# Weight conversion in 32-bit words, a planner that holds the buffers of accumulating DMAs, and 14 weight blocks converted early and kept in DRAM

## The chip, the cores and the metric

One Trainium2 chip, one core of it. The metric is the device time of one execution in microseconds, the median of several runs. Three runs of the kernel before took 594.22, 595.67 and 596.27 us.

## What is computed

Three blocks follow each other on 1536 rows (2 batches of 768) of 512 values. Everything is float32; the weights arrive as float64 numbers, since the host hands their 64 bits over as int64.

```python
# attention: local window of 16, plus 24 block summaries (max of k, mean of v over 32 rows)
scores_all = concat([where(|i-j|<16, q@k.T/8, -1e9), q@k_sum.T/8 + log(32)])
x = softmax(scores_all) @ concat([v, v_sum])        # 8 heads of 64
# first block
h = x @ w_in                                        # 512 -> 2048
x = (maximum(h, 0) + log1p(exp(-abs(h)))) @ w_out   # 2048 -> 512
# second block
out = ((x @ w1) * (x @ w2)) @ w3 @ w_out2           # 512 -> 1024 -> 1024 -> 512
```

## The kernel before

**Numbers and products.** A float32 operand is kept as two fp32r halves, high and low, and each product is three matmuls (`PASSES`, L18; `mm3`, L221). A matmul here is 128x128 by 128x512. The second and third rows chunk of the H and AB products go through a seven-product scheme (`prod`, L666; `keep`, `plus`). `w3 @ w_out2` is multiplied out on the chip first (`w34_mm`, tile `wps`), written to DRAM (`w_d`) and read back.

**Stages.** Attention runs to about 68 us. Then the H and X products (tiles `hps`, `abps`, `xps`, 68 to 354 us in the trace), with softplus between them on DVE and ACT (`S_a` to `S_lo`, L465 to L480), then `w3 @ w_out2` (333 to 396 us, interleaved with the last X products), then the second block (AB, `ops`).

**Weight conversion, one block of 128x512 float64 at a time.** There are 72 blocks (`jobs`): 16 of `w_in`, 16 of `w_out`, 8 of `wo2`, 16 of `w3`, 16 of `w1` and `w2`. SP loads 512 KB into a tile `raw` of 128 x 512 x 2 int32 (`load`, L229): pool `st` with three buffers, or pool `g` for every other block of wo2 and w3. Then:

- `conv_a` (L235): the top three mantissa bits of the low word are moved to the bottom of it. It reads every fourth uint16 and writes every fourth uint16; on ACT (L240, 69 blocks) or DVE (L238, the first 3).
- `conv_b` (L242, DVE L244): the sign bit is put into the neighbouring uint16.
- `conv_c` (L246): high word times a power of two into a tile `cv` (pool of five); ACT (L250) or DVE (L252).
- `conv_d` (L254, DVE L256): shift and bitwise or of `cv` and `raw`; here the `raw` buffer becomes free.
- `conv_e` (L258, ACT L260) and `conv_f` (L262, POOL or DVE L264): high and low half.

**X sums.** Sixteen steps of w_out do not fit one accumulation in PSUM, so four groups of four are copied out to a tile `xo` (`X_copy`, L491: odd ones on ACT, even ones on DVE), and stored to DRAM tile `x_d`: the first group by a plain DMA on SP, the three others by an accumulating DMA issued from POOL (`X_sum`, L498; 36 of them). `X_load` (L506, SP L509) reads the sum back as `x2f`. `xo`, the softplus `tm` and others share a pool `tmp` of four buffers.

**Order.** Nothing is scheduled by hand. Each step is given to a planner, class `Order`, with engine, cost, place, needs and the buffers that it takes and gives back. `order()` lists the steps engine by engine with its own clock and writes each engine's instruction order, which the chip then keeps to. SP issues its DMAs in that order: a DMA that has to wait holds up those behind it. In the planner a buffer that `X_sum` reads is free 0.3 us after the POOL instruction (`LAT`, L22), and `X_load` is ready then. Step names: `l` load, `ca` to `ce` and `c` the conversion, `Xo` copy, `Xs` sum, `Xl` load of the sum, `wm` the w3 product.

The jobs of wo2 and w3 have their conversion placed from `Ph5_7`, late in the H and X stage, on (L891). `X1_6_0` and `X2_15_0` are names of X steps: second rows chunk with block 6, and the last X step of the third chunk.

Of the kernel before, what the change touches and what calls it, by code (L numbers as in the profile page):

```python
# [19 lines left out]
class Order:  # L20
# [9 lines left out]
        self.owner = {}  # L30
        self.extra = {}

    def add(self, name, eng, cost, place, fn, needs=(), take=(), give=(), port=None, table=None, lead=0.0):
        assert name not in self.steps, name
        self.steps[name] = (eng, cost, place, fn, list(dict.fromkeys(d for d in needs if d)), list(take))
        self.extra[name] = (eng == "POOL" if port is None else port, table, lead)
# [62 lines left out]
    def order(self):  # L99
# [25 lines left out]
        while len(out) < len(st):  # L125
            best = None
            for eng, ns in wait.items():
                free = busy_to.get(eng, 0.0)
                cand = []
                for n in ns:  # L130
                    t = max(free, ready[n])
                    port, tab, _ = self.extra[n]
# [30 lines left out]
            port, tab, _ = self.extra[n]  # L163
            if tab:
                table = tab
            for tag, b in take:
                slots[tag].remove(min(slots[tag]))
                head[tag] += 1
            end[n] = t + cost
            busy_to[eng] = end[n]  # L170
            if port:
                port_to = end[n]
            out.append((t, len(out), n))
            for b in gives.get(n, ()):
                slot_end[b] = max(slot_end.get(b, 0.0), end[n] + self.LAT[eng])
                open_users[b] -= 1
                if not open_users[b]:
                    slots[self.owner[b]].append(slot_end[b])
            for m in after[n]:
                lat = self.LAT[eng] if st[m][0] != eng else 0.0 if eng == "PE" else self.SAME  # L180
                ready[m] = max(ready.get(m, 0.0), end[n] + lat)
                left[m] -= 1
                if not left[m]:
                    wait.setdefault(st[m][0], {})[m] = 1
# [6 lines left out]
def fused_kernel(ctx, tc, q, k, kwin, v, vb, w_in, w_out, w1, w2, w3, wo2, mask, sel, ident, out):  # L191
# [43 lines left out]
    def conv_a(kind, i, eng):  # L235
        r = raws[kind, i]
        if eng == "DVE":
            nc.vector.tensor_scalar(r.bitcast(U16)[:, :, 0], r.bitcast(U16)[:, :, 1], 13, None, ALU.logical_shift_right)  # L238
        else:
            nc.scalar.activation(r.bitcast(U16)[:, :, 0], r.bitcast(U16)[:, :, 1], AF.Copy, bias=-(0.5 - 2.0 ** -14), scale=2.0 ** -13)  # L240

    def conv_b(kind, i):  # L242
        r = raws[kind, i]
        nc.vector.tensor_scalar(r.bitcast(U16)[:, :, 1], r.bitcast(U16)[:, :, 3], 0x8000, None, ALU.bitwise_and)  # L244

    def conv_c(kind, i, eng):  # L246
        c = cvs[kind, i] = cv_p.tile([P, D], I32, tag="cv", name="cv")
# [242 lines left out]

    def X_copy(c, g, o):  # L491
        xo[c, g, o] = tmp_p.tile([P, CH], F32, tag="tmp", name="xo")
        if o % 2:
# [258 lines left out]
    for u in range(T):  # L752
# [131 lines left out]
    early = set(jobs[:EARLY])  # L884
    first2 = set(jobs[:3])
    conv_on = lambda j: "DVE" if j in early or j[0] in ("wo2", "w3") and j[1] % 2 else "ACT"
    for j in jobs:
        kind, i, p = j
        n, pl = f"{kind}{i}", at_job[j]
        if kind in ("wo2", "w3"):  # L890
            pl = max(pl, at_["Ph5_7"] + 1.2 * (jobs.index(j) - 32))  # L891
        rt = "g" if kind in ("wo2", "w3") and jobs.index(j) % 2 else "st"
        add("l" + n, "SP", 2.0, pl - 6, lambda kind=kind, i=i, rt=rt: load(kind, i, rt), ("swap" if rt == "g" else None,), [(rt, "r" + n)])
        eng = conv_on(j) if j in first2 else "ACT"
        add("ca" + n, eng, .43 if eng == "DVE" else .66, pl, lambda kind=kind, i=i, eng=eng: conv_a(kind, i, eng), ("l" + n,), port=eng == "DVE")
# [295 lines left out]
```

## Time and profile before

| | us |
|---|---|
| median of three runs | 595.67 |
| the three runs | 594.22 to 596.27 |
| the profiled execution | 592.06 |
| its span, first to last instruction | 590.2 |

Engines' busy share of the span: PE 93%, DVE 73%, ACT 61%, POOL 30%. The mean granted TensorE clock is 0.976 of full speed. The profiled execution is 3.6 us shorter than the median; differences are read from its trace. In the trace a PE row with a bracket shows how long PE sat idle before that row and which engine's instruction ended the wait. A PE that is busy is not always at pace: matmuls that run at the lower clock take twice as long, so a stretch is best read by how many matmuls it holds.

### The profile page before, as it was taken

The numbers are of one execution on the slowest core, as the hardware profiler recorded it, in microseconds if no ns is written. First come the engines' busy times: TensorE is split into PE (matmuls) and PEld (weight loads), VectorE is DVE, ScalarE is ACT, GpSimd is POOL, SyncE is SP. The second block draws the span as 40 slices with busy tenths as digits, with TensorE's granted clock in tenths as the row PEclk, the third lists the DMA queues.
The fourth block names the chain that finished last, engine by engine and source line by source line (L and its number), as shares of the span: only waits on it lengthen the run. The fifth ranks groups of instructions, "written<-read, shape, count | busy, mean of one in ns | idle before, by whom it ended". The sixth has DMA issues, their size and how long they took to land.

```text
span 590.2 us, 8684 instructions
## 1 busy us (share of the span) xinstructions
PE 548.8 (93%) x3118; PEld 442.3 (75%) x3118; DVE 429.4 (73%) x824; ACT 358.3 (61%) x677; POOL 176.9 (30%) x162
## 2 busy tenths in 40 slices
PE   7778899999999999799999788998999999999997
PEld 4566677888887888578877666786887888888885
DVE  4778998886978879667653856799686998753430
ACT  4789878788466886455642958967876433333220
POOL 2465633127132254302312614225645100000000
PEclk9889999999999999879999789999999999999999
DMA  9998744453126457814557589835534010000021
GB/s 311 274 256 211 190 140 137 150 183 108 72 74 141 106 144 142 197 19 58 165 99 159 128 267 272 265 140 191 154 122 123 1 72 0 1 0 1 2 89 53
DMA packets 31442, 76.93 MB, mean 130 GB/s; under 512 B 4104, under 2 KB 4552, under 8 KB 31400
## 3 DMA queue, kind: packets, MB, share of 16 engines
q1 hardware_dynamic: 26216, 66.95, 36.0%
q0 software_dynamic: 5184, 9.44, 11.1%
q8 instruction: 24, 0.39, 0.3%
q14 instruction: 18, 0.15, 0.1%
HBM read 58.45 MB, written 17.92 MB: 129 GB/s over the span
## 4 chain that ended last, share of the span: by engine, by line
PE 56%; DMA 14%; ACT 9%; issue 8%; DVE 8%; POOL 3%; SPq 0%; POOLq 0%; DVEq 0%; ACTq 0%
PE abps L681 19%; PE xps L223 14%; PE ops L223 9%; PE hps L223 8%; DMA raw<-in_w_dram 6%; DMA x_d<-xo 5%; ACT raw L240 3%; ACT s L394 3%; PE abps L223 2%; POOL w L264 2%; DVE cv L256 2%; DMA raw<-in_w_in_dram 2%; DVE raw L244 2%; ACT w L260 1%; PE z_p L838 1%
## 5 line engine op out<-in xcount | busy, mean ns | idle before, releaser
L223 PE MATMUL xps<-gt,w 128*128 128x512 f32 x576 | 146.9, 404 | 12.9 <-ACT gt L477 6.8
L223 PEld LDWEIGHTS xps<-gt,w 128*128 128x128 f32 x576 | 112.0, 196 | 40.1 <-ACT gt L477 8.3
L264 POOL TENSOR_TENSOR w<-cv,w 128x512 fp32r<-128x512 f32 x60 | 88.0, 1473 | 172.9 <-ACT w L260 159.3
L240 ACT ACTIVATE raw<-raw 128x512 uint16<-128x512 uint16 x69 | 94.3, 1385 | 29.0 <-DMA raw<-in_w_dram 17.7
L223 PE MATMUL hps<-xt,w 128*128 128x512 f32 x288 | 70.1, 394 | 1.3 <-DVE gt L480 1.3
L223 PE MATMUL ops<-w,pt 128*128 128x512 f32 x288 | 69.5, 389 | 1.2 <-DVE pt L579 1.2
L244 DVE TENSOR_SCALAR raw<-raw 128x512 uint16<-128x512 uint16 x72 | 60.5, 840 | 12.5 <-ACT raw L240 12.4
L223 PEld LDWEIGHTS hps<-xt,w 128*128 128x128 f32 x288 | 54.2, 190 | 13.8 <-DVE gt L480 2.1
L223 PEld LDWEIGHTS ops<-w,pt 128*128 128x128 f32 x288 | 54.0, 188 | 12.8 <-DVE pt L579 1.6
L256 DVE SCALAR_TENSOR_TENSOR cv<-cv,raw 128x512 int32<-128x512 int32 x72 | 56.8, 788 | 2.8 <-ACT cv L250 0.2
L260 ACT CAST w<-cv 128x512 fp32r<-128x512 f32 x72 | 44.7, 635 | 18.0 <-DVE cv L256 17.5
L687 ACT COPY u<-abps 128x512 f32<-128x512 f32 x42 | 24.7, 591 | 49.4 <-PE abps L681 46.3
L502 POOL DMA_DIRECT2D x_d<-xo x36 | 32.9, 1028 | 72.7 <-DVE xo L496 56.0
L693 DVE TENSOR_TENSOR u<-u,abps 128x512 f32<-128x512 f32 x42 | 28.9, 687 | 29.1 <-ACT u L687 18.3
L223 PE MATMUL wps<-w 128*128 128x512 f32 x192 | 45.0, 392 | 2.9 <-ACT w L260 2.1
L223 PE MATMUL abps<-x2t,w 128*128 128x512 f32 x192 | 46.1, 393 | 1.7 <-POOL w L264 0.9
L223 PEld LDWEIGHTS wps<-w 128*128 128x128 f32 x192 | 35.7, 188 | 11.9 <-ACT w L260 2.6
L223 PEld LDWEIGHTS abps<-x2t,w 128*128 128x128 f32 x192 | 35.5, 188 | 11.2 <-POOL w L264 2.6
L470 ACT ACTIVATE tm<-tm 128x512 f32<-128x512 f32 x48 | 30.0, 636 | 21.0 <-DVE tm L467 20.7
L681 PE MATMUL abps<-t,s 128*128 128x512 f32 x168 | 42.3, 389 | 0.0
L394 ACT ACTIVATE s<-s,sm 128x120 f32<-128x120 f32 x96 | 36.6, 385 | 7.2 <-DVE sm L388 7.1
L681 PEld LDWEIGHTS abps<-t,s 128*128 128x128 f32 x168 | 31.5, 188 | 6.5
(101 smaller groups left out, 846.7 us busy)
## 6 DMA issues: line engine op xcount, KB each, us to landing
raw<-in_w_dram SPq DMA_DIRECT2D x32, 512.0 KB, 4.0
x_d<-xo POOLq DMA_DIRECT2D x36, 256.0 KB, 5.4
raw<-in_w_in_dram SPq DMA_DIRECT2D x16, 512.0 KB, 3.5
raw<-in_w_out_dram SPq DMA_DIRECT2D x16, 512.0 KB, 4.1
vw<-in_v_dram SPq DMA_DIRECT2D x12, 384.0 KB, 9.8
raw<-in_wo_dram SPq DMA_DIRECT2D x8, 512.0 KB, 5.7
kt<-in_k_dram SPq DMA_DIRECT2D x4, 768.0 KB
qt<-in_q_dram SPq DMA_DIRECT2D x12, 256.0 KB, 5.6
```

The lines of the kernel that those rows point to most:

```text
L223: nc.tensor.matmul(ps, lhs(a), rhs(b), start=first and i == 0, stop=last and i == 2)
L240: nc.scalar.activation(r.bitcast(U16)[:, :, 0], r.bitcast(U16)[:, :, 1], AF.Copy, bias=-(0.5 - 2.0 ** -14), scale=2.0 ** -13)
L244: nc.vector.tensor_scalar(r.bitcast(U16)[:, :, 1], r.bitcast(U16)[:, :, 3], 0x8000, None, ALU.bitwise_and)
L256: nc.vector.scalar_tensor_tensor(c, c, 3, r[:, :, 0], ALU.logical_shift_left, ALU.bitwise_or)
L260: nc.scalar.copy(w[:, 0], f(cvs[kind, i]))
L264: eng.tensor_tensor(w[:, 1], f(cvs[kind, i]), f(w[:, 0]), ALU.subtract)
L394: nc.scalar.activation(s[:, e], s[:, e], AF.Exp, bias=sm[:, 0, e:e + 1], scale=-1.0, accum_out=sm[:, 1, e:e + 1])
L470: nc.scalar.activation(tm[c, i], tm[c, i], AF.Softplus)
L502: nc.gpsimd.dma_start(x2_d[4 * c + o], xo[c, g, o], accum_op=ALU.add)
L681: nc.tensor.matmul(ps, w[:, a, (o + kk) * P:(o + kk + 1) * P], rhs(b), start=k in (1, 5, 2) and kk == 0 and n == 0, stop=kk == 1 and n == ...
L687: nc.scalar.copy(tu[z, j, name], bank[z, j, k])
L693: nc.vector.tensor_tensor(tu[z, j, d], tu[z, j, d], bank[z, j, k], ALU.add)
```

## The change

Three things.

1. `conv_a` and `conv_b` write the whole low 32-bit word instead of single uint16. `conv_a` on ACT still reads the uint16 and writes an int32; on DVE it is a 32-bit shift by 29. `conv_b` takes the sign from the high word and combines it with the low word in one two-input instruction.
2. The planner's `add` takes a `tail`. A step's buffers and followers wait for it in the planner's clock: 4.4 us for the accumulating DMAs, 1.0 us for the plain ones of `X_sum`. The copy's engine is taken from a list `XE`, with the same assignment as before.
3. The first 14 jobs of wo2 and w3 are loaded and taken through `conv_a` to `conv_d` between the planned times of `X1_6_0` and `X2_15_0`, evenly spread. The resulting `cv` tile is stored to DRAM (`park`) and read back into another `cv` tile (`unpark`) 4 us ahead of the old place of the conversion; `conv_e` and `conv_f` stay there. Their `raw` tiles are all in pool `st`.

```diff
     def conv_a(kind, i, eng):
         r = raws[kind, i]
         if eng == "DVE":
-            nc.vector.tensor_scalar(r.bitcast(U16)[:, :, 0], r.bitcast(U16)[:, :, 1], 13, None, ALU.logical_shift_right)
+            nc.vector.tensor_scalar(r[:, :, 0], r[:, :, 0], 29, None, ALU.logical_shift_right)
         else:
-            nc.scalar.activation(r.bitcast(U16)[:, :, 0], r.bitcast(U16)[:, :, 1], AF.Copy, bias=-(0.5 - 2.0 ** -14), scale=2.0 ** -13)
+            nc.scalar.activation(r[:, :, 0], r.bitcast(U16)[:, :, 1], AF.Copy, bias=-(0.5 - 2.0 ** -14), scale=2.0 ** -13)
     def conv_b(kind, i):
         r = raws[kind, i]
-        nc.vector.tensor_scalar(r.bitcast(U16)[:, :, 1], r.bitcast(U16)[:, :, 3], 0x8000, None, ALU.bitwise_and)
+        nc.vector.scalar_tensor_tensor(r[:, :, 0], r[:, :, 1], -0x80000000, r[:, :, 0], ALU.bitwise_and, ALU.bitwise_or)
...
+    def park(kind, i):
+        nc.sync.dma_start(pk_d[kind, i], f(cvs[kind, i]))
+    def unpark(kind, i):
+        cvs[kind, i] = cv_p.tile([P, D], I32, tag="cv", name="cv")
+        nc.sync.dma_start(f(cvs[kind, i]), pk_d[kind, i])
...
-                slot_end[b] = max(slot_end.get(b, 0.0), end[n] + self.LAT[eng])
+                slot_end[b] = max(slot_end.get(b, 0.0), end[n] + self.LAT[eng] + tail)
...
-                lat = self.LAT[eng] if st[m][0] != eng else 0.0 if eng == "PE" else self.SAME
+                lat = self.LAT[eng] + tail if st[m][0] != eng else 0.0 if eng == "PE" else self.SAME + tail
...
+    PACE, AHEAD, EARLY, PARK, PA, PB = 3.2, 6.0, 8, 14, "X1_6_0", "X2_15_0"
+    parked = [j for j in jobs if j[0] in ("wo2", "w3")][:PARK]
+    lo, hi = at_[PA], at_[PB]
...
+        pk = j in parked
+        pl2 = lo + (hi - lo) * parked.index(j) / len(parked) if pk else pl
+        rt = "g" if kind in ("wo2", "w3") and jobs.index(j) % 2 and not pk else "st"
...
-        add("cb" + n, "DVE", .43, pl + .1, lambda kind=kind, i=i: conv_b(kind, i), ("ca" + n,), port=True)
+        add("cb" + n, "DVE", .68, pl2 + .1, lambda kind=kind, i=i: conv_b(kind, i), ("ca" + n,), port=True)
...
+        if pk:
+            add("pk" + n, "SP", .7, pl2 + 3, lambda kind=kind, i=i: park(kind, i), ("cd" + n,), (), ("p" + n,))
+            add("up" + n, "SP", .7, pl - 4, lambda kind=kind, i=i: unpark(kind, i), ("pk" + n,), [("cv", "c" + n)])
...
                 add(f"Xs{n}", "POOL" if g else "SP", 1.1 if g else .7, None, lambda c=c, g=g, o_=o_: X_sum(c, g, o_),
-                    (f"Xo{n}", g and f"Xs{c}{g-1}_{o_}"), (), (f"xo{n}",), lead=4 if g == 3 else 0, port=False)
+                    (f"Xo{n}", g and f"Xs{c}{g-1}_{o_}"), (), (f"xo{n}",), lead=4 if g == 3 else 0, port=False, tail=4.4 if g else 1.0)
```

## Rows read from the trace of the kernel before

**Rows 1.** PE in order of time: start us, length us, instruction, count, idle before.
```profile
304.52 12.40 PE L223 MATMUL xps<-gt,w 128*128 128x512 f32 x54
316.76 1.52 PE L681 MATMUL abps<-t,w 128*128 128x512 f32 x6
...
319.48 4.24 PE L223 MATMUL xps<-gt,w 128*128 128x512 f32 x18
328.02 5.36 PE L223 MATMUL xps<-gt,w 128*128 128x512 f32 x12 [4.30 <-ACT gt L477]
...
349.55 4.87 PE L223 MATMUL xps<-gt,w 128*128 128x512 f32 x12 [2.54 <-ACT gt L477]
354.25 11.04 PE L223 MATMUL wps<-w 128*128 128x512 f32 x48
```

**Rows 2.** Windows: length, busy us (instructions) of PE PEld DVE ACT POOL, PEclk, DMA share, GB/s.
```profile
68.00:91.00 23.00, 21.60 (x122) 16.93 (x121) 22.66 (x36) 16.81 (x24) 9.01 (x8) 1.00 0.38 121
91.00:174.00 83.00, 83.00 (x366) 68.74 (x367) 70.60 (x106) 61.16 (x89) 27.86 (x18) 1.00 0.38 127
174.00:196.00 22.00, 20.67 (x90) 16.38 (x89) 17.89 (x32) 14.85 (x23) 6.76 (x6) 1.00 0.51 98
196.00:226.00 30.00, 30.00 (x134) 24.81 (x133) 23.90 (x40) 23.47 (x37) 14.51 (x13) 1.00 0.64 140
226.00:256.00 30.00, 25.40 (x98) 19.90 (x97) 23.29 (x35) 18.08 (x26) 8.91 (x7) 0.86 0.69 158
256.00:291.00 35.00, 35.00 (x152) 28.90 (x151) 22.68 (x37) 17.33 (x28) 6.14 (x6) 0.98 0.38 84
291.00:323.00 32.00, 31.06 (x137) 25.38 (x137) 17.34 (x29) 12.78 (x19) 7.23 (x8) 1.00 0.61 118
323.00:354.00 31.00, 24.05 (x87) 18.34 (x86) 21.86 (x31) 22.56 (x34) 12.05 (x10) 0.83 0.74 199
354.00:396.00 42.00, 39.12 (x169) 31.12 (x168) 32.87 (x46) 34.19 (x45) 14.00 (x13) 1.00 0.73 222
396.00:453.00 57.00, 54.18 (x233) 42.79 (x232) 44.83 (x51) 42.89 (x63) 29.53 (x19) 1.00 0.50 160
453.00:587.00 134.00, 133.06 (x588) 109.83 (x586) 81.23 (x134) 41.26 (x72) 6.78 (x4) 1.00 0.07 24
```

**Rows 3.** DVE in order of time, around 248 us.
```profile
248.20 0.69 DVE L496 COPY xo<-xps 128x512 f32<-128x512 f32 x1 [5.36 <-DMA x_d<-xo]
```

**Rows 4.** DMAs that touch x_d, from issue to landing.
```profile
DMA to landing us min/median/max: 3.7/5.4/8.7
```

**Rows 5.** ACT in order of time, around 323 us.
```profile
323.67 1.33 ACT L240 ACTIVATE raw<-raw 128x512 uint16<-128x512 uint16 x1 [8.29 <-DMA raw<-in_w_dram]
```

**Rows 6.** Waits of SP's own queue: us in total, times, longest us.
```profile
SPq L509 <- DMA x_d<-xo: 38.8, 7, 14.1
SPq L231 <- PE xps L223: 37.5, 2, 37.1
```

**Rows 7.** SP's queue in order of time, around 316 us.
```profile
316.16 0.47 SPq L231 DMA_DIRECT2D raw<-in_w_dram  x1
```

**Rows 8.** Groups of instructions: count, busy us, mean ns of one, idle before.
```profile
L240 ACT ACTIVATE raw<-raw 128x512 uint16<-128x512 uint16 x69 | 94.3, 1385 | 29.0 <-DMA raw<-in_w_dram 17.7 <-DMA raw<-in_w_out_dram 5.2 <-DMA raw<-in_wo_dram 3.2
L244 DVE TENSOR_SCALAR raw<-raw 128x512 uint16<-128x512 uint16 x72 | 60.5, 840 | 12.5 <-ACT raw L240 12.4
L256 DVE SCALAR_TENSOR_TENSOR cv<-cv,raw 128x512 int32<-128x512 int32 x72 | 56.8, 788 | 2.8 <-ACT cv L250 0.2
L250 ACT ACTIVATE cv<-raw 128x512 f32<-128x512 f32 x52 | 35.7, 692 | 0.0
```

**Rows 9.** DMA issues: count, KB each, median us to landing.
```profile
w_d<-w34o SPq DMA_DIRECT2D x8, 256.0 KB, 4.5
w34r<-w_d SPq DMA_DIRECT2D x8, 256.0 KB, 2.7
```

More of the change, by code (lines that the diff above doesn't have):

```diff
@@ L31, in __init__, with add @@
         self.extra = {}
-    def add(self, name, eng, cost, place, fn, needs=(), take=(), give=(), port=None, table=None, lead=0.0):
+    def add(self, name, eng, cost, place, fn, needs=(), take=(), give=(), port=None, table=None, lead=0.0, tail=0.0):
         assert name not in self.steps, name
         self.steps[name] = (eng, cost, place, fn, list(dict.fromkeys(d for d in needs if d)), list(take))
-        self.extra[name] = (eng == "POOL" if port is None else port, table, lead)
+        self.extra[name] = (eng == "POOL" if port is None else port, table, lead, tail)
         for t, b in take:
@@ L131, in order @@
                     t = max(free, ready[n])
-                    port, tab, _ = self.extra[n]
+                    port, tab, _, tail = self.extra[n]
                     if port:
@@ L162, in order @@
             del wait[eng][n]
-            port, tab, _ = self.extra[n]
+            port, tab, _, tail = self.extra[n]
             if tab:
@@ L214, in fused_kernel @@
     w34_d = dr.tile([8, P, D], F32, name="w34_d")
+    pk_d = {("wo2", i): dr.tile([P, D], F32, name=f"pk_wo2{i}") for i in range(8)}
+    pk_d.update({("w3", i): dr.tile([P, D], F32, name=f"pk_w3{i}") for i in range(16)})
     x2_d = [dr.tile([P, CH], F32, name=f"x2_d{r}") for r in range(12)]
@@ L492, in X_copy @@
         xo[c, g, o] = tmp_p.tile([P, CH], F32, tag="tmp", name="xo")
-        if o % 2:
+        if XE[o] == "ACT":
             nc.scalar.copy(xo[c, g, o], xps[c, g, o])
@@ L762, in fused_kernel @@
     WO = (0, 4, 1, 5, 2, 6, 3, 7, 8, 12, 9, 13, 10, 14, 11, 15)
+    XE = ("DVE", "ACT", "DVE", "ACT")
     SEQ = (1, 5, 6, 2, 7, 4, 3)
@@ L865, in fused_kernel @@
     jobs += [(f"w{m+1}", i, "wo" if i < 3 else ("wi", "g")[m] if i == 3 else "b") for i in range(8) for m in range(2)]
-    PACE, AHEAD, EARLY = 3.2, 6.0, 8
+    PACE, AHEAD, EARLY, PARK, PA, PB = 3.2, 6.0, 8, 14, "X1_6_0", "X2_15_0"
     first = {}
@@ L889, in fused_kernel @@
         n, pl = f"{kind}{i}", at_job[j]
+        pk = j in parked
         if kind in ("wo2", "w3"):
             pl = max(pl, at_["Ph5_7"] + 1.2 * (jobs.index(j) - 32))
-        rt = "g" if kind in ("wo2", "w3") and jobs.index(j) % 2 else "st"
-        add("l" + n, "SP", 2.0, pl - 6, lambda kind=kind, i=i, rt=rt: load(kind, i, rt), ("swap" if rt == "g" else None,), [(rt, "r" + n)])
+        pl2 = lo + (hi - lo) * parked.index(j) / len(parked) if pk else pl
+        rt = "g" if kind in ("wo2", "w3") and jobs.index(j) % 2 and not pk else "st"
@@ L894, in fused_kernel @@
+        add("l" + n, "SP", 2.0, pl2 - 6, lambda kind=kind, i=i, rt=rt: load(kind, i, rt), ("swap" if rt == "g" else None,), [(rt, "r" + n)])
         eng = conv_on(j) if j in first2 else "ACT"
-        add("ca" + n, eng, .43 if eng == "DVE" else .66, pl, lambda kind=kind, i=i, eng=eng: conv_a(kind, i, eng), ("l" + n,), port=eng == "DVE")
-        add("cb" + n, "DVE", .43, pl + .1, lambda kind=kind, i=i: conv_b(kind, i), ("ca" + n,), port=True)
+        add("ca" + n, eng, .43 if eng == "DVE" else .66, pl2, lambda kind=kind, i=i, eng=eng: conv_a(kind, i, eng), ("l" + n,), port=eng == "DVE")
@@ L897, in fused_kernel @@
+        add("cb" + n, "DVE", .68, pl2 + .1, lambda kind=kind, i=i: conv_b(kind, i), ("ca" + n,), port=True)
         eng = conv_on(j)
-        add("cc" + n, eng, .43 if eng == "DVE" else .66, pl + .3, lambda kind=kind, i=i, eng=eng: conv_c(kind, i, eng),
-            ("l" + n,), [("cv", "c" + n)], port=eng == "DVE")
-        add("cd" + n, "DVE", .69, pl + .4, lambda kind=kind, i=i: conv_d(kind, i), ("cc" + n, "cb" + n), (), ("r" + n,), port=True)
+        add("cc" + n, eng, .43 if eng == "DVE" else .66, pl2 + .3, lambda kind=kind, i=i, eng=eng: conv_c(kind, i, eng),
+            ("l" + n,), [("cv", ("p" if pk else "c") + n)], port=eng == "DVE")
@@ L901, in fused_kernel @@
+        add("cd" + n, "DVE", .69, pl2 + .4, lambda kind=kind, i=i: conv_d(kind, i), ("cc" + n, "cb" + n), (), ("r" + n,), port=True)
+        if pk:
+            add("pk" + n, "SP", .7, pl2 + 3, lambda kind=kind, i=i: park(kind, i), ("cd" + n,), (), ("p" + n,))
+            add("up" + n, "SP", .7, pl - 4, lambda kind=kind, i=i: unpark(kind, i), ("pk" + n,), [("cv", "c" + n)])
         add("ce" + n, "ACT", .62, pl + .5, lambda kind=kind, i=i, p=p: conv_e(kind, i, pools[p]),
-            ("cd" + n, "swap2" if p in "bc" else "swap" if p == "g" else None), [(p, n)])
+            ("up" + n if pk else "cd" + n, "swap2" if p in "bc" else "swap" if p == "g" else None), [(p, n)])
@@ L986, in fused_kernel @@
                 n = f"{c}{g}_{o_}"
-                add(f"Xo{n}", "ACT" if o_ % 2 else "DVE", .6, None, lambda c=c, g=g, o_=o_: X_copy(c, g, o_),
+                add(f"Xo{n}", XE[o_], .6, None, lambda c=c, g=g, o_=o_: X_copy(c, g, o_),
                     (f"X{c}_{4*g+3}_{o_//2}",), [("tmp", f"xo{n}")], (f"x{n}",))
                 add(f"Xs{n}", "POOL" if g else "SP", 1.1 if g else .7, None, lambda c=c, g=g, o_=o_: X_sum(c, g, o_),
-                    (f"Xo{n}", g and f"Xs{c}{g-1}_{o_}"), (), (f"xo{n}",), lead=4 if g == 3 else 0, port=False)
+                    (f"Xo{n}", g and f"Xs{c}{g-1}_{o_}"), (), (f"xo{n}",), lead=4 if g == 3 else 0, port=False, tail=4.4 if g else 1.0)
                 if g == 3:
```

## The prediction

> **What bounds the kernel now.** I read the busy time in windows first, since PE is busy nearly everywhere and the question is where it is not at pace. A steady stretch gives the pace: 54 matmuls start at 304.52 and the next group at 316.76, 12.24 us or 0.2267 us each [rows 1]. Multiply the count of each window by that and compare with its length [rows 2]. From 91 to 174 us, 196 to 226, 256 to 291 and 453 to 587 the product is the length or within 1 us of it (588 x 0.2267 = 133.3 of 134): PE is the bound there and nothing in this change takes a matmul away. The time that can be won lies in the other windows:
>
> - 174 to 196: 22.0 - 90 x 0.2267 = 1.6 us
> - 226 to 256: 30.0 - 98 x 0.2267 = 7.8
> - 291 to 323: 32.0 - 137 x 0.2267 = 0.9
> - 323 to 354: 31.0 - 87 x 0.2267 = 11.3
> - 354 to 396: 42.0 - 169 x 0.2267 = 3.7
> - 396 to 453: 57.0 - 233 x 0.2267 = 4.2
> - 68 to 91: PE idle 23.0 - 21.6 = 1.4, with DVE busy 22.66 of 23 us; other shapes are among these matmuls, so I count idle time alone.
>
> Together 30.9 us. That is the most that any edit of the waits can give. A few matmul records may be missing from the trace, so each term is a little high rather than low.
>
> Then I looked up what ends each gap. **226 to 256:** DVE sat 5.36 us until an accumulating DMA `x_d<-xo` had landed, then copied the next `xo` [rows 3]: all four `tmp` buffers were tied up, and PE had no free PSUM bank for the next X group. These DMAs take 3.7 to 8.7 us to land, median 5.4 [rows 4]; the planner frees the buffer 0.3 us after the issue, so it put nothing else there. After the gap the granted clock is down: 0.86 over the window [rows 2]. **323 to 354:** ACT sat 8.29 us until a raw weight block came [rows 5]; behind that instruction in ACT's order stood the softplus that PE needed, and PE was idle 4.30 us before 328.02 [rows 1]. The block was issued only at 316.16 [rows 7], because SP stood before it on `X_load`, up to 14.1 us, waiting for the accumulating DMAs [rows 6]. Earlier SP had stood 37.1 us on one raw load of pool `g`, whose buffer an X step still held [rows 6]: the wo2 and w3 blocks were meant to come early and couldn't. The twelve matmuls from 328.02 then take 5.36 us where 0.2267 us each would be 2.7: they run at 1.2 instead of 2.4 GHz after the idle time (0.83 over the window, rows 2). The same again at 349.55, idle 2.54 and then 354.25 - 349.55 = 4.70 for twelve [rows 1]. So a gap of 2.54 costs 2.54 + 4.70 - 2.72 = 4.5 us. **354 to 453:** ACT is busy 34.2 of 42 us and 42.9 of 57 [rows 2], with conversions in the way of the copies.
>
> **The change part by part.**
>
> *32-bit writes.* `conv_a` on ACT takes 1385 ns as a uint16 write [rows 8]. The nearest row for a 512-element ACT copy that reads the same 8-byte stride is L250, 692 ns, with a contiguous write. A strided 32-bit ACT write doesn't occur in this trace. So the new cost is between 692 and 1385; I take 0.70, as the same read stride at 692 leaves the uint16 store as what differs most. That is 69 x 0.69 = 47.6 us of ACT time over the kernel, nearly all beside PE's work; it reaches the end only in the windows above. `conv_b` becomes a two-input instruction like `conv_d`: 788 against 840 ns [rows 8], 72 x 0.05 = 3.7 us of DVE. Bounds: 0 (no gain) to 0.15 us more each if two strided inputs from one tile cost extra, 11 us of DVE, hidden where DVE has room. The planner's own costs (0.66 and now 0.68) come nearer to what the chip takes, so its orders should fit better. I give this no term.
> [...]
>
> *Start, 68 to 91.* DVE-bound; three `conv_a` and some ten `conv_b` get a little shorter. Of the 1.4 us of idle I take 0.5 (0 to 1.4).
>
> *The tail.* It moves no data faster. In its clock the planner now sees the `tmp` buffers as taken for 4.4 us more and can put other DVE and PE work into that time, and it no longer lists `X_load` before its data are there, so SP issues weight loads first. Windows 174 to 196 and 226 to 256 hold 9.4 us of loss from the buffers. Four `tmp` buffers remain four, and the real landing (5.4, up to 8.7, rows 4) is longer than 4.4 + 0.3, so I take 5 of 9.4 (0 to 9.4).
>
> *Parking.* Each of 14 blocks gives up its load of 512 KB and four instructions late, and gets them early; added are a store and a read of 256 KB on SP. By like transfers these land in 4.5 and 2.7 us [rows 9]. Late side: the block needs only `conv_e` and `conv_f` after its read. With SP free of the wait on `X_load` and of the `g` buffer, and 14 x (1.385 + 0.69) = 29 us of ACT gone from the stretch after about 300 us, the late windows 291 to 354 (12.2 us of loss) should shrink most: I take 9 (5 to 12). Window 354 to 396 still converts ten w3 and wo2 blocks and the first of w1 and w2: 2.5 of 3.7 (0 to 3.7). Window 396 to 453 has only the shorter `conv_a`: 2 of 4.2 (0 to 4.2).
> Early side: from 196 to 354 us DVE is busy 109.1 of 158 us and ACT 94.2 (sums of rows 2). Parked work adds 14 x (0.79 + 0.79) = 22 us on DVE, less what of it was already in that stretch, and 14 x 1.4 = 20 on ACT, less 0.69 for each of the other blocks. On average that fits, 83% of DVE at most. Locally it is tight: 196 to 226 has DVE at 23.9 of 30 and would get three blocks, 4.7 us. What hides the early work is this room; without it each late softplus shows up as a gap of a few us. The 14 stores, 3.7 MB, add to a DMA share of 0.64 to 0.69. SP order: a store waits for `conv_d`, and the next `w_in` or `w_out` load is queued behind it; the parked blocks also share the three `st` buffers. The same-order cost of one or two such gaps I put at 3 us (0 to 12).
>
> Sum: 0.5 + 5 + 9 + 2.5 + 2 = 19; less 3 is 16 us. Against the profiled execution 592.06 - 16 = 576.1. That execution lies 3.6 us under the median of 595.67; the same gain from the median gives **579.7 us**. Terms at their best and no new gap give 30.8, 564.9.
>
> **The rivals.**
>
> *The buffers stay the bound.* The planner can reorder, but PE can't start an X group without banks, and loads and stores on SP's queue run beside the accumulating DMAs. If they land at 7 to 8.7 us instead of 5.4 [rows 4], the tail term is 0 and new waits take 6. Then 0.5 + 0 + 9 + 2.5 + 2 - 6 = 8 us: 588. For it: DMA share 0.69 in 226 to 256, where the longest wait is. Against: most of the 14 loads are only spread out, not added.
> The Trainium skill states in "DMA: Bandwidth & Descriptors", section "Issuing engines are not separate DMA queues", that DMAs of all issuing engines run on the same 16 engines and interleave; that is what this rival needs, and the spread 3.7 to 8.7 us agrees with it.
>
> *Everything fits.* The planner with true costs closes nearly all gaps: 25 us or more, 570 or below. For it: the windows without such waits are at pace to within 1 us. Against: the order is only as good as its clock, and 396 to 453 is crowded on three engines.
>
> *The narrow write isn't what is slow.* `conv_a` stays near 1385. Then 354 to 453 gives nothing (4.5 us less), and the parked work costs ACT 29 us early, 2 more of gaps: 9.5 us won, 586.
>
> *The early work stalls the H and X stage.* Store behind `conv_d`, weight load behind the store, softplus and copies behind conversions on a DVE at 80%: PE waits between 196 and 320 us, where it is at pace now. One gap of 2.5 us costs 4.5 with the clock that follows. Six of them are 27 us instead of the 3 charged: 595.67 - 19 + 27 = 604. It decides from the fifth gap on (4 x 4.5 = 18 against 19 won).
>
> **How the numbers follow.** The forecast (572 to 585) 0.55; buffers stay the bound 0.14; everything fits 0.13; narrow write 0.08; stalls 0.10, of which some end near 596. A measurement of this kernel can tell about 0.3%, 1.8 us. Faster by more than that (below 593.9): 0.86; within it 0.05; slower 0.09. The range 568 to 592 leaves out the slow rival and the last corner of the best case.
>
> **What would show it.** Right: L240 near 0.7 us; no 14 us wait of SP on `x_d<-xo`; PE at 0.2267 us per matmul from 291 to 354; a granted clock of 1.00 in 226 to 256. Wrong: PE gaps in 196 to 226 or 256 to 320 ended by DVE or ACT; SP waiting on DVE `cv` at the stores; landings of x_d above 5.4; L240 unchanged; the wait for `x_d<-xo` on DVE still some 5 us.

## The result, and the profile after

The changed kernel takes 573.34 us (median of four runs, 569.85 to 575.27); the kernel before, run beside it, 594.94. The ratio is 0.9636, 95% interval 0.9572 to 0.9701: 21.6 us less, where 16 were forecast (579.7) and the range was 568 to 592. The profiled execution after is the longest of its four, 575.27 us with a span of 573.5; against the profiled execution before, 592.06 and 590.2, that is 16.8 us of time and 16.7 of span, where 16 were forecast. The other 4.8 us of the median lie between executions; no trace shows them. In two of the comparisons further down one execution was in a slower state (581.20 us of e6_u16_in_after, 585.30 of e12_park18_early): the ratios leave it out, the medians in us count it.

The windows of the changed kernel, cut near the same points of the work as [rows 2]; the counts of matmuls differ, by 38 in the last one. What is compared is therefore each window's loss, its length less its own count at pace (columns as there: length, busy us and instructions of PE, PEld, DVE, ACT, POOL, granted clock, DMA share, GB/s):

```profile
70.00:91.00 21.00, 20.36 (x118) 16.68 (x119) 19.41 (x35) 12.74 (x20) 8.56 (x6) 1.00 0.41 127
174.00:196.00 22.00, 21.33 (x92) 16.68 (x91) 20.58 (x33) 12.41 (x23) 4.93 (x5) 1.00 0.53 108
196.00:226.00 30.00, 29.42 (x129) 23.71 (x128) 23.59 (x40) 18.96 (x34) 9.55 (x9) 1.00 0.70 173
226.00:256.00 30.00, 27.89 (x121) 22.14 (x120) 24.77 (x39) 17.70 (x32) 11.44 (x11) 1.00 0.86 217
256.00:291.00 35.00, 34.83 (x152) 28.12 (x152) 30.85 (x54) 21.86 (x39) 8.48 (x9) 1.00 0.61 158
291.00:323.00 32.00, 30.08 (x126) 24.36 (x126) 20.54 (x31) 18.11 (x33) 12.41 (x12) 0.95 0.89 240
323.00:347.00 24.00, 23.94 (x106) 19.52 (x105) 21.37 (x28) 15.95 (x29) 12.74 (x13) 1.00 0.93 275
347.00:386.00 39.00, 36.15 (x153) 29.42 (x152) 34.16 (x38) 23.86 (x42) 15.79 (x10) 0.96 0.74 228
386.00:447.00 61.00, 61.00 (x271) 50.52 (x270) 43.69 (x55) 37.64 (x65) 30.69 (x20) 1.00 0.42 127
```

Read with 0.2267 us per matmul, as in the prediction, the loss of each is: idle time at the start 0.6 (1.4 before), then 1.1 (1.6), 0.8 (0), 2.6 (7.8), 0.5 (0), 3.4 (0.9), 0 (11.3), 4.3 (3.7), 0 (4.2). Together 13.3 us where there were 30.9, so 17.6 won. The first H matmul starts 2.5 us later here (70.64 against 68.1), which goes against it: 15.1 of the 16.7 us of span. The other 1.6 us were not followed up.

PE in order of time, the places that answer to [rows 1], and the two largest gaps left from 91 us on (start us, length us, instruction, count, idle before):

```profile
248.18 3.69 PE L225 MATMUL xps<-gt,w 128*128 128x512 f32 x15 [0.31 <-DVE xo L505]
...
305.60 1.85 PE L690 MATMUL abps<-xt,s 128*128 128x512 f32 x6 [1.92 <-ACT u L696]
...
318.22 6.96 PE L225 MATMUL xps<-gt,w 128*128 128x512 f32 x30
...
361.04 23.66 PE L225 MATMUL wps<-w 128*128 128x512 f32 x96 [2.85 <-ACT w34o L546]
```

The idle 4.30 and 2.54 us of [rows 1] are gone: from 323 to 347 us the window loses nothing. At 248 us PE waits 0.31 us.

Groups of instructions (count, busy us, mean ns of one, idle before them and what ended it), against [rows 8]:

```profile
L246 DVE SCALAR_TENSOR_TENSOR raw<-raw 128x512 int32<-128x512 int32 x72 | 57.0, 792 | 6.8 <-ACT raw L242 6.6
L242 ACT ACTIVATE raw<-raw 128x512 int32<-128x512 uint16 x69 | 46.5, 675 | 31.2 <-DMA raw<-in_w_dram 9.6 <-DMA raw<-in_wo_dram 8.5 <-DMA raw<-in_w_out_dram 7.7
```

`conv_a` halved, from 1385 to 675 ns, and `conv_b` went from 840 to 792.

Waits of SP's queue (us in total, times, longest), against [rows 6]:

```profile
SPq L261 <- DVE cv L258: 71.1, 11, 13.1
SPq L518 <- DMA x_d<-xo: 24.2, 7, 6.2
```

The landing of all DMAs that touch `x_d`, against [rows 4]:

```profile
DMA to landing us min/median/max: 2.6/6.0/12.0
```

The reads of the sum still wait, in shorter pieces, and a new wait stands on the same queue: SP stood 71.1 us on `conv_d` at the stores of the parked blocks. The DMAs on `x_d` land later than before (median 6.0 for 5.4, longest 12.0 for 8.7; the accumulating ones alone 6.1 and 12.0), with the DMA share of 226 to 256 us up from 0.69 to 0.86. Even so DVE's wait at the place of [rows 3] fell from 5.36 to 2.42 us (DVE in order of time):

```profile
247.43 0.69 DVE L505 COPY xo<-xps 128x512 f32<-128x512 f32 x1 [2.42 <-DMA x_d<-xo]
```

### The profile page after: what moved, and what is told of

The parts are those of the page before. It is cut to its first block, busy times and chain, and to the rows that moved or that the text cites. A ratio compares the mean times of both kernels' runs of the same rounds, so it can differ in the third digit from the quotient of the medians.

```text
span 573.5 us, 8749 instructions
## 1 busy us (share of the span) xinstructions
PE 543.4 (95%) x3118; PEld 440.9 (77%) x3118; DVE 428.2 (75%) x824; ACT 318.6 (56%) x677; POOL 176.3 (31%) x162
## 4 chain that ended last, share of the span: by engine, by line
PE 41%; DMA 7%; issue 7%; ACT 2%; POOL 2%; DVE 1%; SPq 0%; POOLq 0%; DVEq 0%; ACTq 0%
PE abps L690 15%; PE ops L225 11%; PE abps L225 8%; PE wps L225 4%; PE xps L225 4%; DMA x_d<-xo 3%; POOL w L273 1%; DMA raw<-in_wo_dram 1%; DMA raw<-in_w_dram 1%; DMA cv<-pk_wo 1%; POOL x_d L511 1%; ACT w L269 1%; DVE cv L258 0%; ACT raw L242 0%; ACT xo L503 0%
## 5 line engine op out<-in xcount | busy, mean ns | idle before, releaser
L225 PE MATMUL xps<-gt,w 128*128 128x512 f32 x576 | 141.4, 394 | 1.3 <-DVE xo L505 1.0
L273 POOL TENSOR_TENSOR w<-cv,w 128x512 fp32r<-128x512 f32 x60 | 91.7, 1542 | 155.2 <-ACT w L269 138.4
L225 PEld LDWEIGHTS xps<-gt,w 128*128 128x128 f32 x576 | 108.6, 190 | 26.9 <-DVE gt L489 2.5
L242 ACT ACTIVATE raw<-raw 128x512 int32<-128x512 uint16 x69 | 46.5, 675 | 31.2 <-DMA raw<-in_w_dram 9.6
L246 DVE SCALAR_TENSOR_TENSOR raw<-raw 128x512 int32<-128x512 int32 x72 | 57.0, 792 | 6.8 <-ACT raw L242 6.6
L258 DVE SCALAR_TENSOR_TENSOR cv<-cv,raw 128x512 int32<-128x512 int32 x72 | 54.9, 763 | 4.6 <-ACT cv L252 2.0
L479 ACT ACTIVATE tm<-tm 128x512 f32<-128x512 f32 x48 | 30.1, 633 | 30.2 <-DVE tm L476 30.0
L225 PEld LDWEIGHTS wps<-w 128*128 128x128 f32 x192 | 37.1, 194 | 11.2 <-ACT w34o L546 3.3
L225 PE MATMUL abps<-x2t,w 128*128 128x512 f32 x192 | 44.5, 389 | 0.0
```

The lines of the kernel that those rows point to most:

```text
L225: nc.tensor.matmul(ps, lhs(a), rhs(b), start=first and i == 0, stop=last and i == 2)
L242: nc.scalar.activation(r[:, :, 0], r.bitcast(U16)[:, :, 1], AF.Copy, bias=-(0.5 - 2.0 ** -14), scale=2.0 ** -13)
L246: nc.vector.scalar_tensor_tensor(r[:, :, 0], r[:, :, 1], -0x80000000, r[:, :, 0], ALU.bitwise_and, ALU.bitwise_or)
L273: eng.tensor_tensor(w[:, 1], f(cvs[kind, i]), f(w[:, 0]), ALU.subtract)
L479: nc.scalar.activation(tm[c, i], tm[c, i], AF.Softplus)
```

## The experiments

Ratios are to the kernel before in the same comparison, with 95% intervals; its medians were 594.94 us for the changed kernel, 593.89 for e1 to e4, 592.98 for e5 to e8 and 593.88 for e9 to e12. A ratio is not the quotient of the two medians, and the two differ by up to 0.3%. A difference in us below is one of medians, unless it is said to be by the ratios.

| kernel | words | tail | parking | us | ratio |
|---|---|---|---|---|---|
| changed kernel | yes | 4.4, both halves | 14 | 573.34 | 0.9636 [0.9572, 0.9701] |
| e1_words | yes | no | no | 587.59 | 0.9894 [0.9865, 0.9924] |
| e2_tail | no | 4.4, both halves | no | 580.52 | 0.9790 [0.9739, 0.9842] |
| e5_park | no | no | 14 | 596.17 | 1.0045 [1.0018, 1.0071] |
| e3_no_park | yes | 4.4, both halves | no | 576.87 | 0.9735 [0.9671, 0.9800] |
| e4_no_tail | yes | no | 14 | 583.04 | 0.9830 [0.9776, 0.9884] |
| e6_u16_in_after | no | 4.4, both halves | 14 | 576.07 | 0.9693 [0.9642, 0.9744] |
| e7_tail_buffers | no | 4.4, buffers only | no | 590.81 | 0.9967 [0.9943, 0.9992] |
| e8_tail_followers | no | 4.4, followers only | no | 580.68 | 0.9799 [0.9766, 0.9831] |
| e9_tail_reads | no | 4.4, last sum's followers only | no | 582.99 | 0.9808 [0.9779, 0.9836] |
| e10_no_buffer_tail | yes | 4.4, followers only | 14 | 574.49 | 0.9648 [0.9603, 0.9694] |
| e11_tail64 | yes | 6.4, both halves | 14 | 572.82 | 0.9645 [0.9614, 0.9676] |
| e12_park18_early | yes | 4.4, both halves | 18, from earlier on | 578.28 | 0.9727 [0.9696, 0.9758] |

### One part alone

**The 32-bit words alone**, in the order of the kernel before:

```diff
-            nc.scalar.activation(r.bitcast(U16)[:, :, 0], r.bitcast(U16)[:, :, 1], AF.Copy, ...)
+            nc.scalar.activation(r[:, :, 0], r.bitcast(U16)[:, :, 1], AF.Copy, ...)
```

(and the same for `conv_a` on DVE and `conv_b`, as in the change)

> The kernel before with the 32-bit writes of conv_a and conv_b alone; the planner's costs are left, so every engine's order is that of the kernel before. Theory of the prediction: ACT time falls by some 47 us, but the gaps of 226 to 256 and 323 to 354 us are ended by DMAs and stay; 2 to 6 us faster, about 591 us. Rival, the conversions' speed is what was won: most of the 21 us, 578 us or less.

587.59 us, 6.3 less. The group of `conv_a` in this kernel (columns as above):

```profile
L240 ACT ACTIVATE raw<-raw 128x512 int32<-128x512 uint16 x69 | 46.1, 674 | 33.2 <-DMA raw<-in_w_dram 21.0 <-DMA raw<-in_w_out_dram 6.2 <-DMA raw<-in_wo_dram 3.3
```

Its ACT and then its PE in order of time (start us, length us, instruction, count, idle before):

```profile
324.74 0.67 ACT L240 ACTIVATE raw<-raw 128x512 int32<-128x512 uint16 x1 [7.76 <-DMA raw<-in_w_dram]
```

```profile
328.53 5.79 PE L223 MATMUL xps<-gt,w 128*128 128x512 f32 x12 [3.20 <-ACT gt L477]
```

ACT lost 48 us of work (94.3 to 46.1) and the kernel 6: ACT waits in the same place for the same load, 7.76 us where it was 8.29 [rows 5], and PE behind it 3.20 where it was 4.30 [rows 1]. What it won shows elsewhere: the second late gap is down from 2.54 to 0.37 and 0.68 us (at 348.71 and 349.89), and the window 396 to 453 loses 1.0 us (247 matmuls) instead of 4.2. Expected were 2 to 6 us with both gaps staying; a little more came, and the second gap nearly went.

**The tail alone**, with the uint16 writes and no parking:

```diff
+    lat = self.LAT[eng] + tail if st[m][0] != eng else ...
+    slot_end[b] = max(slot_end.get(b, 0.0), end[n] + self.LAT[eng] + tail)
+    add(f"Xs{n}", ..., tail=4.4 if g else 1.0)
```

> The kernel before with the planner's tail alone: uint16 writes, no parking. Theory: the read of the sums no longer stands ahead of weight loads on SP and the copies into tmp are planned around the landing; 5 to 10 us faster, about 587 us, the wait of DVE for x_d shorter than 5.4 us. Rival, the tail frees no buffer: within 2 us of the kernel before, 595 us.

580.52 us, 13.4 less: the largest of the three by far, and more than the 5 to 10 that were expected of it.

**Parking alone:**

```diff
-    PACE, AHEAD, EARLY = 3.2, 6.0, 8
+    PACE, AHEAD, EARLY, PARK, PA, PB = 3.2, 6.0, 8, 14, "X1_6_0", "X2_15_0"
```

(with `park`, `unpark` and their steps; no tail, uint16 writes)

> The kernel before with parking alone: uint16 writes, tail 0. Theory, parking relieves the late conversions and is worth 4 to 6 us wherever it is added (it was 4.6 us on top of the 32-bit writes): 588 to 590 us. Rival, with the slow uint16 conversions the early work has no room on ACT and the gain is 0 or less: 594 us or more.

596.17 us: slower by 3.2, the interval just above 1. The theory, 588 to 590 us, failed, and its rival came in. ACT of this kernel in order of time, then PE:

```profile
332.73 1.05 ACT L523 CAST x2t<-x2f 128x1024 fp32r<-128x1024 f32 x1 [7.31 <-DMA x2f<-x_d]
333.69 0.62 ACT L479 ACTIVATE tm<-tm 128x512 f32<-128x512 f32 x1
```

```profile
336.91 4.64 PE L225 MATMUL xps<-gt,w 128*128 128x512 f32 x12 [3.15 <-ACT gt L486]
...
383.38 24.14 PE L225 MATMUL wps<-w 128*128 128x512 f32 x96 [6.85 <-ACT w34o L546]
```

The late gap is still there, with another instruction in front. No load holds ACT now, but the cast of the sum that has been read back (`x2_hi`, L523): 7.31 us, and behind it again the softplus (L479) that PE waits for. Before the `w3` products a further 6.85 us open up: by the chain of the trace, behind a weight load that left at 371.56, right after a read of the sum at 371.14.

### One part taken away

**No parking:**

```diff
-    PACE, AHEAD, EARLY, PARK, PA, PB = 3.2, 6.0, 8, 14, "X1_6_0", "X2_15_0"
+    PACE, AHEAD, EARLY, PARK, PA, PB = 3.2, 6.0, 8, 0, "X1_6_0", "X2_15_0"
```

> The changed kernel with no block parked: 32-bit writes and tail. Theory: the late windows (291 to 400 us) keep part of their loss, since all 24 blocks of wo2 and w3 are again converted there; 5 to 9 us slower than the changed kernel, about 580 us. Rival, parking is worth nothing once the other two are in: 573 us.

576.87 us. Parking, worth a loss alone, is worth 0.9735 - 0.9636, 1% or 5.9 us by the ratios (3.5 by the medians; 5 to 9 were expected), beside the two others; the two intervals overlap, so its size there is loose.

**No tail:**

```diff
-    ..., port=False, tail=4.4 if g else 1.0)
+    ..., port=False, tail=0.0)
```

> The changed kernel with tail 0: 32-bit writes and parking. Theory: the buffers of the accumulating DMAs are again planned as free at once; PE waits of 4 to 6 us for a copy into tmp come back and SP stands on the reads of the sums; 5 to 8 us slower than the changed kernel, about 580 us. Rival, the tail is worth nothing: 573 us.

583.04 us: without the tail 1.9% of the 3.6% are lost, 11.5 us by the ratios and more than expected. ACT of this kernel in order of time, then PE:

```profile
317.74 1.05 ACT L523 CAST x2t<-x2f 128x1024 fp32r<-128x1024 f32 x1 [7.24 <-DMA x2f<-x_d]
```

```profile
321.91 0.50 PE L225 MATMUL xps<-gt,w 128*128 128x512 f32 x1 [3.06 <-ACT gt L486]
```

As with parking alone: the cast of the sum, 7.24 us, ahead of the softplus (318.69). The two waits that the expectation named did not come back. At 248 us DVE waits 3.97 us for `x_d`, but PE only 0.26, and not for a copy into `tmp`; SP's waits on the reads of the sum are 25.5 us in total and 6.8 at the longest, against 24.2 and 6.2 with the tail. So these shorter waits of SP, a sign that the prediction named for being right, do not come from the tail.

**uint16 writes in the changed kernel**, its order untouched:

```diff
-            nc.scalar.activation(r[:, :, 0], r.bitcast(U16)[:, :, 1], AF.Copy, ...)
+            nc.scalar.activation(r.bitcast(U16)[:, :, 0], r.bitcast(U16)[:, :, 1], AF.Copy, ...)
```

> The changed kernel with the uint16 writes of before in conv_a and conv_b, the order being that of the changed kernel: tail and parking. Theory, the parts add: 4 us slower than the changed kernel, 577 us. Rival, the planned order relies on the short conversions and breaks without them: 583 us or more.

576.07 us: the words are worth about 0.6% here, 3.4 us by the ratios, though again the intervals overlap. As with the words alone, most of some 48 us of ACT time is beside PE's work.

### Which half of the tail

**Buffers only** (against the kernel with the tail alone):

```diff
-                lat = self.LAT[eng] + tail if st[m][0] != eng else 0.0 if eng == "PE" else self.SAME + tail
+                lat = self.LAT[eng] if st[m][0] != eng else 0.0 if eng == "PE" else self.SAME
```

> The kernel before with half of the tail: in the planner the buffers of the accumulating DMAs are taken 4.4 us longer, but the steps that follow (the reads of the sums, the next sum) are ready at once. Theory A, the wait for tmp buffers was what cost: nearly all of the 13 us, 581 to 583 us. Theory B, the late reads of the sums were: 590 to 594 us.

590.81 us, 2.2 less than before. SP's queue of this kernel in order of time, then ACT, then PE:

```profile
316.09 0.33 SPq L518 DMA_DIRECT2D x2f<-x_d  x1
316.47 1.79 SPq L233 DMA_DIRECT2D raw<-in_w_dram  x1
```

```profile
323.79 1.33 ACT L242 ACTIVATE raw<-raw 128x512 uint16<-128x512 uint16 x1 [8.21 <-DMA raw<-in_w_dram]
324.88 0.67 ACT L479 ACTIVATE tm<-tm 128x512 f32<-128x512 f32 x1
```

```profile
328.14 5.79 PE L225 MATMUL xps<-gt,w 128*128 128x512 f32 x12 [4.22 <-ACT gt L486]
```

The load is issued 0.4 us after the read of the sum that stands before it on SP, as in [rows 7]; ACT waits 8.21 us for it, the softplus comes behind, PE is idle 4.22 us. DVE's wait of [rows 3] at the copy is gone; the longest for `x_d` from 170 to 262 us is 1.38 us, at a softplus step. The window 226 to 256 loses 3.5 us (117 matmuls) instead of 7.8, but 174 to 196 now loses 4.5 (77 matmuls) instead of 1.6. This half does what it should at its place, and it is worth two microseconds.

**Followers only** (buffers free at once):

```diff
-                slot_end[b] = max(slot_end.get(b, 0.0), end[n] + self.LAT[eng] + tail)
+                slot_end[b] = max(slot_end.get(b, 0.0), end[n] + self.LAT[eng])
```

> The kernel before with the other half of the tail: the steps that follow an accumulating DMA are ready 4.4 us later in the planner, the buffers free at once as before. Theory A (buffers): 590 to 594 us and the DVE wait for x_d at 242 us stays at some 5 us. Theory B (reads of the sums): 581 to 585 us and the gap before 328 us is gone.

580.68 us, 12.3 less: nearly all of the 13.4 that the tail brings alone. The late gaps are gone, while DVE still waits 4.65 us for the buffers (at 247.10) and PE behind it; the window 226 to 256 still loses 7.3 us. PE of this kernel:

```profile
247.84 2.07 PE L225 MATMUL xps<-gt,w 128*128 128x512 f32 x4 [2.98 <-DVE xo L505]
```

**Only the read of the sum is told later:** as the last, with the 4.4 us on the last accumulating DMA of a group alone.

```diff
-    ..., port=False, tail=4.4 if g else 1.0)
+    ..., port=False, tail=4.4 if g == 3 else 0.0)
```

> The kernel before with a quarter of the tail: only the last of the three accumulating DMAs delays its follower by 4.4 us, which is the read of the sum; buffers are free at once and one sum follows another at once. Theory B narrowed, the reads of the sums are all of it: 579 to 583 us, as with all followers delayed. Rival, the spacing of one sum behind another matters too: 586 us or more.

582.99 us, at the edge of the 579 to 583 expected: 10.9 less by one number in the planner that only `X_load` sees; everything else that changes is what the planner makes of it. SP's queue of this kernel in order of time:

```profile
302.37 0.80 SPq L233 DMA_DIRECT2D raw<-in_w_dram  x2
316.93 6.79 SPq L518 DMA_DIRECT2D x2f<-x_d  x4
```

The waits of that queue (us in total, times, longest):

```profile
SPq L518 <- DMA x_d<-xo: 38.7, 7, 13.7
SPq L233 <- PE xps L225: 38.1, 3, 37.3
```

ACT of this kernel in order of time, then PE:

```profile
314.96 1.36 ACT L242 ACTIVATE raw<-raw 128x512 uint16<-128x512 uint16 x1
...
320.09 0.63 ACT L479 ACTIVATE tm<-tm 128x512 f32<-128x512 f32 x1 [3.34 <-DVE tm L476]
...
336.62 0.69 ACT L479 ACTIVATE tm<-tm 128x512 f32<-128x512 f32 x1
...
344.67 1.05 ACT L523 CAST x2t<-x2f 128x1024 fp32r<-128x1024 f32 x1
```

```profile
320.52 6.96 PE L225 MATMUL xps<-gt,w 128*128 128x512 f32 x30
```

The prediction followed only the first of the two late gaps to its end. For the second, at 349.55, ACT of the kernel before shows the cast of the sum and a `conv_a`, and SP the load of that block, which left behind two more reads of the sum (339.57):

```profile
344.97 1.05 ACT L514 CAST x2t<-x2f 128x1024 fp32r<-128x1024 f32 x1 [5.21 <-DMA x2f<-x_d]
...
347.71 1.35 ACT L240 ACTIVATE raw<-raw 128x512 uint16<-128x512 uint16 x1 [0.66 <-DMA raw<-in_w_dram]
```

```profile
340.46 0.43 SPq L231 DMA_DIRECT2D raw<-in_w_dram  x1
```

Here is the mechanism. SP waits as long as before: 38.7 us for the sums, 13.7 at the longest, against 38.8 and 14.1 [rows 6], and 37.3 for the buffer of pool `g`. What changed is what stands behind the wait. From 280 us on, the sixth weight load left at 316.16 in the kernel before, after the first read of the sum [rows 7]; here two leave at 302.37, the fifth and the sixth, and then the reads. On ACT a `conv_a` runs at 314.96 without a wait, still ahead of the softplus at 320.09 (by the order of the loads it is that block's; the trace does not name blocks). At the second gap the softplus, at 336.62, now comes ahead of the cast of a sum, at 344.67; the same two steps by count came the other way round in the kernel before (cast 344.97, softplus 345.92). PE has no gap from 323 to 354 us.

### The changed kernel, varied

**No tail on the buffers, in the changed kernel** (the edit of the followers-only kernel):

```diff
-                slot_end[b] = max(slot_end.get(b, 0.0), end[n] + self.LAT[eng] + tail)
+                slot_end[b] = max(slot_end.get(b, 0.0), end[n] + self.LAT[eng])
```

> The changed kernel with the tail on the followers alone, the buffers of the accumulating DMAs being free at once in the planner. Theory B: no difference that shows, 571 to 576 us, though the DVE wait for x_d at 242 us is longer. Rival, with the other gaps closed the buffers now count: 578 us or more.

574.49 us: no difference, and DVE's wait is a little longer, 2.80 us instead of 2.42. The part of the change that stands in its title is worth nothing here that can be measured.

**A tail of 6.4 us**, nearer to the landing of 6.0:

```diff
-    ..., port=False, tail=4.4 if g else 1.0)
+    ..., port=False, tail=6.4 if g else 1.0)
```

> The changed kernel with a tail of 6.4 instead of 4.4 us, which with the planner's 0.3 us covers the median landing of 6.0 us. Theory: a planner that is closer to the chip wins a little more, 568 to 573 us, and SP stands on the reads for less than 24 us. Rival, the landing's mean matters little, and the order merely changes: 573 to 577 us.

572.82 us: the same time, but not the same kernel. PE of it, in order of time:

```profile
187.95 4.61 PE L225 MATMUL hps<-xt,w 128*128 128x512 f32 x12 [2.44 <-DVE gt L489]
...
362.53 22.05 PE L225 MATMUL wps<-w 128*128 128x512 f32 x96 [0.61 <-ACT w34o L546]
```

The gap ahead of the `w3` products is 0.61 us instead of 2.85, and the window 291 to 323 loses 0.9 us instead of 3.4. Against that, 174 to 226 loses 8.9 us (74 and 116 matmuls) instead of 1.9, at a granted clock of 0.92 and 0.94. The two kernels lose in different places, and the sums come out alike. SP's waits on the reads are 23.3 us, as expected, though 9.7 at the longest.

**Parking 18 blocks, and from earlier on:**

```diff
-    PACE, AHEAD, EARLY, PARK, PA, PB = 3.2, 6.0, 8, 14, "X1_6_0", "X2_15_0"
+    PACE, AHEAD, EARLY, PARK, PA, PB = 3.2, 6.0, 8, 18, "Ph1_2", "X2_15_0"
```

> The changed kernel with 18 instead of 14 blocks parked, spread from the start of the first product group (some 135 us) instead of X1_6_0. Theory, the late loads and the DMA engines at full share from 340 to 360 us bound the wait before 361 us, and parking more and earlier relieves both: 568 to 572 us. Rival, the early conversions meet a DVE that is busy 8 to 9 tenths there and the gain is 0 or less: 574 us or more.

578.28 us, 0.9% slower than the changed kernel by the ratios, whose intervals just overlap; against the kernel with the tail of 6.4, in the same comparison, they are apart. Its profiled execution is the shortest of the six, 576.05 us, so the trace shows little of this difference. The rival came in. The gap ahead of the `w3` products stays, 2.24 us instead of 2.85, and new ones open where PE was at pace, the largest 1.39 us at 143.71.

## Why the prediction was right, and where its reasons were not

**The size.** 16 us were forecast by the profiled execution and 16.8 came. The account by windows carried it: what was won lay in windows that the prediction named. That the total came so close is partly luck. Term by term (below) the misses are -3.1, +2.2, +1.7, +0.7, +0.3 and -0.2 us, and they nearly cancel. The best case is 30.7 by its own terms and not 30.8, which changes nothing.

**Buffers, 174 to 256: 5 of 9.4 taken, 5.7 won** (1.1 + 2.6 left). The granted clock of 226 to 256 rose from 0.86 to 1.00, as foretold. The cause was given as the buffers' tail. Alone it does close most of the gap at its place (7.8 to 3.5 us), but a new loss before it takes most of that back, and the kernel gains 2.2 us. In the changed kernel it can be left out: the window 226 to 256 then loses 2.1 us (123 matmuls). With words and parking and no tail at all it loses 5.3 (109 matmuls). So the other parts shorten this window as well; which of them does how much was not separated.

**Late windows, 291 to 354: 9 of 12.2 taken, 8.8 won.** The size is right, by luck, and the cause is wrong: this is the step that failed. The sum booked it under parking, by less ACT work and "SP free of the wait on `X_load` and of the `g` buffer". Parking alone lost 3.2 us and left the gap of 3.15; halving ACT's `conv_a` left it at 3.20; moving the reads of the sum closed it while SP stood as long on both waits (38.7 and 37.3 us against 38.8 and 37.1). The tail paragraph did have the right sentence, that SP issues weight loads first, and put no number on it. The kernels without the followers' tail show that this sentence was half of it. In front of the softplus stood a `conv_a` whose load was behind the reads on SP (the kernel before, words alone, buffers only), or the cast of the sum (with parking: 7.31 and 7.24 us), or, at the second gap of the kernel before, both. Either hangs on the sum. Parking without the tail does put the load ahead of the reads, and then the cast holds ACT. With the followers' tail the planner puts the load ahead of the reads on SP and the cast behind the softplus on ACT. In the changed kernel, SP and then ACT in order of time:

```profile
308.02 0.38 SPq L233 DMA_DIRECT2D raw<-in_w_dram  x1
...
314.91 5.47 SPq L518 DMA_DIRECT2D x2f<-x_d  x4
```

```profile
317.79 0.63 ACT L479 ACTIVATE tm<-tm 128x512 f32<-128x512 f32 x1 [3.71 <-DVE tm L476]
...
322.04 1.99 ACT L523 CAST x2t<-x2f 128x1024 fp32r<-128x1024 f32 x2
```

What decides is the order on these two queues; ACT was only 61% busy in the kernel before.

**Window 354 to 396: 2.5 of 3.7 taken, 0.6 lost** (347 to 386: 4.3). This term is wrong. ACT ahead of the gap at 361 us, in the changed kernel:

```profile
358.83 0.65 ACT L242 ACTIVATE raw<-raw 128x512 int32<-128x512 uint16 x1 [1.52 <-DMA raw<-in_w_dram]
359.39 1.12 ACT L269 CAST w<-cv 128x512 fp32r<-128x512 f32 x2
360.41 1.06 ACT L546 COPY w34o<-wps 128x512 f32<-128x512 f32 x2
```

The prediction counted ACT's busy time here; ACT now waits 5.6 us for raw blocks, in four pieces from 350 to 359 us (1.36, 1.28, 1.46 and 1.52), and the copy that frees PE's banks is behind them. The chain that ends at this gap (start us, length us, what; an accumulating DMA, the read of its sum on SP, a weight load, PE):

```profile
342.98 8.34 DMA x_d<-xo
...
351.34 0.33 SPq L518
...
351.75 7.05 DMA raw<-in_w_dram
...
361.04 2.98 PE wps L225 x7
```

It is the pattern of [rows 7] once more: the load left right after a read that had waited for a sum. It then took 7.05 us to land, where the median of these loads is 4.6, at a DMA share of 0.93 from 323 to 347 us ([rows 2] had 0.74 for 323 to 354). The share alone does not make the gap: with the tail of 6.4 us it is 0.95 there, four loads leave together from 347.61 on, ahead of the next read at 358.97, and the gap is 0.61 us.

**Window 396 to 453: 2 of 4.2 taken, all 4.2 won.** PE is at pace from 386 us on. **Start:** 0.8 of idle time won for 0.5 taken, though the first H matmul came 2.5 us later, at 70.64. In the traces of the experiments it comes between 67.84 and 69.94; whether the rest is the change's doing was not separated.

**Early work: 3 charged.** The windows 196 to 226 and 256 to 291 lost 1.3 us that they did not lose before, and 291 to 323 went from 0.9 to 3.4, with a gap of 1.92 us at 305.60 ended by ACT: a `conv_a` of a wo2 block, all of which are parked, had waited 3.67 us for its load ahead of the copy that PE needed. That is 3.8, of which the 2.5 are already counted in the 8.8 above. Three of the signs named for being wrong came: such a gap, SP's wait for `cv` at the stores (71.1 us) and landings above 5.4 us. None of them told right from wrong here.

**The narrow write.** It was what was slow: 675 ns against the 0.70 taken. `conv_b` was taken at 0.79 and took 0.792. The Trainium skill, "ScalarE: Activation LUTs", section "What ACT_TABLE_LOAD costs", gives one element per cycle for every function, fp32 and bf16 alike, and with immediate scale and bias 186 ns + 0.833 ns per element, an estimate of 613 ns here. The 32-bit form comes near to it (675); the uint16 form, at 1385, does not. With the same read, the word size of the write was worth 710 ns.

**The rivals.** "The buffers stay the bound" had its condition, landings of 7 to 8.7 us, met by some DMAs only (median 6.1, longest 12.0 us), and fell, as DVE's wait shrank. The Trainium skill, "DMA: Bandwidth & Descriptors", section "Issuing engines are not separate DMA queues", has all these DMAs share the same engines; the later landings at a higher DMA share agree with it. "The early work stalls" has its like in parking alone (3.2 us slower than the kernel before) and in the 18 earlier blocks (4.9 slower than the changed kernel), far from the 27 that it priced. "Everything fits" did not come, but the time is nearer to its 570 us than to the forecast: 13.3 of 30.9 us of loss are left. "The narrow write isn't what is slow" fell with the 675 ns.

**The parts together.** Alone they give 6.3 + 13.4 - 3.2 = 16.5 us; together 21.6. Parking is a loss only when it stands alone. Beside the tail it takes the ratio from 0.9790 to 0.9693, and beside the words, with no tail, from 0.9894 to 0.9830 (587.59 to 583.04 us); in each pair the intervals overlap a little. So either of the two others is enough to turn it into a gain. Why is not shown: e5's rival, no room on ACT beside the uint16 conversions, doesn't explain the gain beside the tail with the same uint16 conversions. Taking `X_load` off SP's queue was not tried, though the chain ahead of 361 us still runs through it. No kernel here beat the changed one; the 6.4 us tail is equal to it in time.

## What to carry to other kernels

An order that is fixed ahead of time is as good as the planner's idea of when a DMA's data are there: in this kernel, giving the landing time to the DMA's readers won 12.3 us, and giving it to its buffers 2.2. On an engine that works in order, ask of each long wait what stands behind it, and move that; the wait itself may stay as long as it was. A right total does not confirm its terms: only the kernels with half of one part showed which line of the change had won the time. Nor do equal times mean equal kernels, as the tail of 6.4 us shows; read where each loses.

## What was not expected of the hardware

A strided uint16 write costs ACT twice what a 32-bit write with the same stride and the same uint16 read costs: 1385 against 675 ns for 128x512 (674 in the kernel that changes nothing else). On DVE a two-input 32-bit instruction over strided words (792 ns) is no dearer than the one-input uint16 form that it replaces (840). Accumulating DMAs of 256 KB landed later in the kernels that park blocks, which move more beside them: medians of 6.1 to 6.8 us at a DMA share of 0.69 to 0.79 from 174 to 356 us, against 5.2 to 6.1 at 0.59 to 0.65 in those that do not.
